# Softplus and the exponentials of one kernel through a single ScalarE table

## The chip, the cores and the metric

The kernel runs on one NeuronCore of a Trainium2 chip. The metric is device microseconds of one execution; before the change the median of 3 runs is 1014.26 us (1013.38 to 1015.45).

## What is computed

Three stages follow each other. The attention works on 4 batches of 8 heads, 576 tokens, head size 64:

```python
scores = q @ k.T / 8, causal; a = exp(scores - max); a /= a.sum() + 1e-9
local = a @ v
phi(x) = where(x > 0, x, exp(x) - 1) + 1
mem = (phi(q) @ M_prev) / (phi(q) . z_prev + 1e-6)
x = g * mem + (1 - g) * local              # g = sigmoid(beta), per head
```

The heads side by side give 2304 tokens of 512. The first layer is `h = x @ w_in` (512 to 2048), `g = max(h, 0) + log1p(exp(-|h|))`, which is softplus(h), and `g @ w_out` (2048 to 512). The second layer is `h = x @ w_in2`, a quotient of a cubic in h by `1 + |b0||h| + |b1| h^2`, and `@ w_out2`. All data is float32.

## The kernel before

Nothing is issued where it is written. Every call of an engine is recorded as an `Op` of a `Program` (line 392 of the profile is the one place that issues nearly all of them, which is why rows are told apart by tiles, not by lines). `Program.order` (a list scheduler) then walks through all recorded steps with modelled durations (`cost`), latencies between engines, a key per step (lower goes first) and dependencies by memory range; it fixes the order of each engine once, and also chooses the engine where a step was recorded with `flex` as possible on several. The order that comes out is static: an engine that waits holds back what stands behind it.

The attention runs in seven passes (`PASSES`) over batch and token range: three passes "L" (tokens 0 to 255, two units of 4 heads), one "F" (all 576 tokens, four units of 2 heads), three "H" (tokens 256 to 575, four units of 2 heads). The first three attention passes are done in float32 (`attention32`), the others with operands split into two float16 halves (`attention`, with `pre`, `scores`, `norm`). In a unit, `masked` (one DVE instruction) writes the masked scores and their minimum with the sign turned, `expo` (ACT) takes the exponential with that minimum as bias and sums it up, `norm` scales the rows and splits them, DMA transposes turn them, PE multiplies by v. A ring of three PSUM banks (`s_bank`) holds the scores.

The first layer goes over blocks of tokens, and over 8 pairs (`Q`) of 256 hidden columns each. `g1(Q)` multiplies into one PSUM bank `hf` and takes the activation; `g2(Q)` multiplies the result by `w_out`, three pairs later (`LAG` = 3). The first two blocks (16 pairs, 2 x 256 columns) are float32; the other 80 pairs (48 of 2 x 160 columns, 24 of 2 x 192, 8 of 2 x 256) take three float16 products. Attention of the next pass runs beside the first layer of the last one; PE takes steps of the attention ahead of those of the first layer.

The activation of a float16 pair takes, before: `Relu` (ACT or DVE) into SBUF; `Abs` with scale, `Exp`, `Ln` on ACT, in the bank; on DVE a multiply and add of the two parts, in the bank; a copy to float16 (the high half, ACT or DVE) and on DVE the difference (the low half). A float32 pair takes Relu, Abs, Exp, Ln and one DVE addition.

Weights are float64 in HBM and are turned to float32 by three bit steps of DVE on 128 x 512 (`bits`); 11 pieces of the second layer's weights are instead turned by `bits_abs`: two DVE steps, `Sign` and `Abs` on ACT, a product on POOL. Scales for the split come from sums of absolute values (`pre`, `w_scale`).

The second layer (`h1`, `h2_`) runs over 96 steps F of 128 hidden columns on 384 tokens each; each takes `Abs`, `Square`, `Ln` and `Exp` on ACT. `x2load` computes its constants from `fa`, `fb`, `fr`, which `consts2` makes from `a` and `b` with `Abs`, `Ln`, `Exp`. `w_split` splits its weights.

Of the kernel before, what the change touches and what calls it, by code (L numbers as in the profile page):

```python
# [24 lines left out]
LAG = 3  # L25

# [23 lines left out]
SIGN = ((0,), (0,))  # L50
SIGN2 = ((1,), (0, 0, 1))
# [5 lines left out]
SIGN3 = (0, 0, 1)  # L57
# [3 lines left out]
EXP = 0x7F800000  # L61

# [106 lines left out]
class Program:  # L169
# [5 lines left out]
    def __init__(self):  # L175
        self.ops = []
        self.access = {}
        self.key = 0.0
        self.pkey = 0.0
        self.bulk = False  # L180
        self.bias = BIAS
        self.cur = None

    def add(self, eng, name, fn, kw, writes=()):
# [29 lines left out]
        op.dma = dma  # L214
        if ported:
            op.port.add(eng)
# [205 lines left out]
def attn_moe_moe2(ctx, tc, q, k, v, m_prev, z_prev, beta, w1i, w1o, w2i, w2o, ca, cb, out):  # L422
# [147 lines left out]
    one = const.tile([128, 1], F32, name="one")  # L570
    pcnt = [0]
# [15 lines left out]
    def pow2(bound, n, name, bufs=3, out=None):  # L587

        cl = tn(name + "c", n, bufs) if out is None else out
        ts(cl, bound, 2.0 ** -13, 2.0 ** -53, ALU.mult, ALU.max)  # L590
        return cl, scale_of(cl, n, name, bufs)
# [131 lines left out]

    def pre(u):
# [3 lines left out]
        for i, src in enumerate((u.rq, u.rk, u.rv)):  # L728
            x = src.rearrange("p g d -> p (g d)")
            n = width(x)  # L730
            A.activation(out=u.nnf[:, 0:n], in_=x, func=AF.Abs, accum_out=acc[:, i:i + 1])
        A.activation(out=u.zt, in_=u.rq, func=AF.Relu, scale=-1.0)
        A.activation(out=u.ph, in_=u.zt, func=AF.Exp, scale=-1.0)
        stt(u.ph, u.rq, 0.0, u.ph, ALU.max, ALU.add)
# [6 lines left out]
        ts(rn, rn, 1e-6, None, ALU.add)  # L741
# [5 lines left out]
        ts(cl[:, 0:3], top[:, 0:3], 2.0 ** -13, 2.0 ** -53, ALU.mult, ALU.max)  # L747
# [22 lines left out]
        ts(tm, ut, m.e, None, ALU.mult)  # L770
# [35 lines left out]
    def expo(x, least, acc):  # L806
        A.activation(out=x, in_=x, func=AF.Exp, bias=least, scale=-1.0, accum_out=acc)


    def scores(u, e):  # L810
# [3 lines left out]
        if u.p.qts[0] == 0:  # L814
# [5 lines left out]
            for t in (1, 0):  # L820
                x = u.pr[e, t]
                masked(x, x, mask[:, 384 - t * 128:512], u.c, nm[:, t:t + 1])
                expo(x, nm[:, t:t + 1], sm[:, t:t + 1])
        for t in (2, 3):
# [6 lines left out]
            masked(x, x, mask[:, 384 - t * 128:512], u.c, nm[:, 0:1])  # L831
            expo(x, nm[:, 0:1], sm[:, t:t + 1])

    def scores_first(u):
# [4 lines left out]
        for t, es in ((1, (0, 1)), (1, (2, 3)), (0, (0, 1, 2, 3))):  # L839
# [5 lines left out]
            for e in es:  # L845
                x, c = u.pr[e, t], 4 * t + e
                masked(x, x, mask[:, 384 - t * 128:512], u.c, nm[:, c:c + 1])
                expo(x, nm[:, c:c + 1], sm[:, c:c + 1])

    def scores_last(u):  # L850
# [7 lines left out]
        masked(ds[1], ds[1], mask4, u.c, nm[:, 1:2], nm[:, 0:1])  # L858
        for j in range(2):
# [15 lines left out]
    def norm(u, e):  # L875
# [4 lines left out]
        ts(r[:, t0:t1], sm[:, t0:t1], 1e-9, u.isa[:, e:e + 1], ALU.add, ALU.mult)  # L880
# [123 lines left out]
    def attention32(u):  # L1004
# [12 lines left out]
        for t in (1, 0):  # L1017
# [7 lines left out]
            for e in range(4):  # L1025
# [3 lines left out]
                expo(x, nm[:, i:i + 1], sm[:, i:i + 1])  # L1029
        yield  # L1030
        A.activation(out=u.zt, in_=u.rq, func=AF.Relu, scale=-1.0)
        A.activation(out=u.ph, in_=u.zt, func=AF.Exp, scale=-1.0)
        stt(u.ph, u.rq, 0.0, u.ph, ALU.max, ALU.add)
# [5 lines left out]
        ts(rn, rn, 1e-6, None, ALU.add)  # L1039
# [4 lines left out]
        for t in (1, 0):  # L1044
            sl = slice(4 * t, 4 * t + 4)
            stt(r[:, sl], sm[:, sl], 1e-9, iog[:, h0:h0 + 4], ALU.add, ALU.mult)
# [37 lines left out]
    def xgroup(p):  # L1084
# [18 lines left out]
        g.csg = tn("xcsg")  # L1103
        ts(g.csg, g.c, g.sg, None, ALU.mult)
# [27 lines left out]
    def bits_abs(r, dst, sgn, acc=None):  # L1132


        hi, lo = r[:, :, 1], r[:, :, 0]
        m = dst.bitcast(U32)
        A.activation(out=sgn, in_=hi.bitcast(F32), func=AF.Sign)
        ts(m, hi, 3, 0xC0000000, ALU.logical_shift_left, ALU.bitwise_xor)
        stt(m, lo, 29, m, ALU.logical_shift_right, ALU.bitwise_or)
        A.activation(out=dst, in_=dst, func=AF.Abs, **({} if acc is None else {"accum_out": acc}))  # L1140
        G.tensor_tensor(out=dst, in0=dst, in1=sgn, op=ALU.mult)

    def w_scale(acc, name):
        m = tn(name + "m", 1, 1)
        V.tensor_reduce(out=m, in_=acc, axis=AX.X, op=ALU.max)
        bd, s = pow2(pmax(m, 1), 1, name, 1)
# [17 lines left out]
    def g1(Q):  # L1164
# [4 lines left out]
        r = vw(RR[Q % 2], (2 * tb,), F32)  # L1169
        if j < NF32:  # L1170

            for f in range(2):
# [73 lines left out]
    V.memset(one, 1.0)  # L1246
    V.memset(qe, 1.0)
# [86 lines left out]
    def w1_bits(which, pc):  # L1334
        r = w1_raw(which, pc)
        dst = w1_place(which, pc + 2, True)
        if SIGN[which][pc % len(SIGN[which])]:
# [334 lines left out]
```

## Time and profile before

| | |
|---|---|
| median of 3 runs | 1014.26 us (1013.38 to 1015.45) |
| span of the profiled execution | 1014.2 us, 22841 instructions |
| busy, share of the span | PE 95%, DVE 88%, ACT 82%, POOL 45% |
| granted TensorE clock, mean | 0.985 |

No time of the profiled execution other than its span is given; the span is within 0.1 us of the median of the runs. In the profile the float32 first layer shows from 43 to 234 us, the float16 first layer from 208 to 626 us, attention until 542 us and the second layer from about 623 us to the end. Names: "arena" is the one large SBUF tile, "tiny" holds columns of one to ten numbers, "bank" is PSUM, "a", "w", "lt", "gr" are further SBUF tiles.

### The profile page before, as it was taken

The page shows a single profiled execution, that of the slowest core. Times are in us where ns is not written, and L with a number is a line of the kernel's source. Part 1 is how long each engine was busy: PE and PEld are TensorE (multiplying, and loading weights), DVE is VectorE, ACT ScalarE, POOL GpSimd, SP SyncE. Part 2 cuts the span into 40 slices and gives each one's busy share as a digit, 9 for nine tenths or more (in the row PEclk, how much of TensorE's full clock was granted, in tenths as well). Part 3 has the DMA queues.
Part 4 walks back from the last instruction along what each step waited for, and adds up shares of the span by engine and source line. Part 5 has one row for each costly group of instructions (what it writes and reads, how often), then busy time and mean ns, then how long its engine had stood idle before and what let it go on. Part 6 is the DMA issues. An engine that isn't in the chain of part 4 may idle for free. (4 is left out here: it accounts for less than half of the span.)

```text
span 1014.2 us, 22841 instructions
## 1 busy us (share of the span) xinstructions
PE 959.6 (95%) x8256; PEld 696.0 (69%) x8256; DVE 893.1 (88%) x2193; ACT 826.8 (82%) x1934; POOL 455.6 (45%) x516
## 2 busy tenths in 40 slices
PE   7779999999979999999899999899999999999998
PEld 6547688788769888888888998445555555555553
DVE  6999778988899988899878999988989889798886
ACT  4886988888869999899887888867888787887875
POOL 3121566873342243342325343655655455555443
PEclk9969999999989999999999999989999999999999
DMA  9997347568689979998998664000001000000000
GB/s 249 317 227 200 66 102 145 123 121 158 130 170 168 153 144 163 184 182 193 209 282 267 219 207 144 1 1 32 32 1 63 1 32 32 1 32 2 32 1 31
DMA packets 249889, 122.08 MB, mean 120 GB/s; under 512 B 219184, under 2 KB 225328, under 8 KB 249776
## 3 DMA queue, kind: packets, MB, share of 16 engines
q1 hardware_dynamic: 249776, 120.63, 51.4%
q8 instruction: 64, 1.05, 0.4%
q14 instruction: 49, 0.40, 0.1%
HBM read 65.54 MB, written 15.73 MB: 80 GB/s over the span
## 5 line engine op out<-in xcount | busy, mean ns | idle before, releaser
L392 PE MATMUL bank<-arena,w 128*128 128x160 f16 (+3 forms) x4288 | 414.8, 256 | 12.0 <-DVE arena L392 7.3
L392 PE MATMUL bank<-arena 128*128 128x384 f16 (+10 forms) x2852 | 355.6, 299 | 24.3 <-DVE arena L392 8.6
L392 PEld LDWEIGHTS <-w 128*128 128x128 f16 x3840 | 292.8, 98 | 29.9 <-issue 18.7
L392 ACT ACTIVATE arena<-bank,tiny 128x384 f32<-128x384 f32 (+8 forms) x504 | 276.3, 587 | 41.4 <-PE bank L392 34.6
L392 PEld LDWEIGHTS <-arena 128*128 128x128 f16 (+1 forms) x2464 | 165.8, 105 | 119.8 <-issue 29.8
L392 POOL TENSOR_TENSOR arena<-arena 128x384 f32<-128x384 f32 (+8 forms) x165 | 167.9, 1021 | 166.3 <-ACT arena L392 104.1
L392 PE MATMUL bank<-arena,gr 128*128 128x512 f16 x864 | 202.8, 380 | 1.2 <-POOL gr L392 1.1
L392 PEld LDWEIGHTS <-gr 128*128 128x128 f16 x864 | 84.5, 98 | 95.5 <-POOL gr L392 2.5
L392 POOL TENSOR_TENSOR gr<-arena,gr 128x384 f16<-128x384 f32 x96 | 90.6, 944 | 103.6 <-issue 81.2
L392 POOL TENSOR_SCALAR arena<-arena,tiny 128x512 f16<-128x512 f32 (+9 forms) x94 | 71.6, 768 | 102.2 <-DVE tiny L392 31.9
L392 ACT ACTIVATE bank<-bank,tiny 128x320 f32<-128x320 f32 (+5 forms) x192 | 103.3, 545 | 14.5 <-DVE tiny L392 9.5
L392 ACT ACTIVATE bank<-bank 128x320 f32<-128x320 f32 (+2 forms) x208 | 104.8, 504 | 1.6
L392 ACT ACTIVATE arena<-bank 128x320 f16<-128x320 f32 (+5 forms) x147 | 72.2, 501 | 29.6 <-PE bank L392 16.6
L392 PEld LDWEIGHTS bank<-arena,w 128*128 128x128 f32 x448 | 83.1, 190 | 12.4 <-issue 1.5
L392 DVE SCALAR_TENSOR_TENSOR arena<-arena,tiny 128x512 f16<-128x512 f32 (+5 forms) x101 | 89.8, 903 | 1.8 <-POOL arena L392 1.1
L392 DVE SCALAR_TENSOR_TENSOR bank<-bank,tiny,lt 128x384 f32<-128x384 f32 x96 | 59.6, 621 | 34.0 <-ACT lt L392 32.3
L392 ACT ACTIVATE lt<-arena,qe 128x384 f32<-128x384 f32 x96 | 59.0, 614 | 32.6 <-POOL arena L392 31.0
L392 DVE SCALAR_TENSOR_TENSOR arena<-arena,qe,lt 128x384 f32<-128x384 f32 x96 | 76.0, 791 | 0.7 <-ACT lt L392 0.7
L392 DVE SCALAR_TENSOR_TENSOR arena<-bank,tiny,arena 128x384 f16<-128x384 f32 (+4 forms) x112 | 64.0, 591 | 8.9 <-ACT arena L392 8.4
L392 DVE TENSOR_SCALAR tiny<-tiny 128x1 f32<-128x1 f32 (+8 forms) x349 | 64.5, 208 | 6.4 <-ACT bank L392 5.1
L392 DVE CUSTOM_DVE_ANT_0 bank<-bank,mask,tiny 128x384 f32<-128x384 f32 (+4 forms) x112 | 66.8, 605 | 2.4 <-PE bank L392 2.0
L392 PEld LDWEIGHTS bank<-arena 128*128 128x128 f32 (+3 forms) x412 | 43.2, 168 | 29.2 <-ACT arena L392 8.1
(122 smaller groups left out, 1143.3 us busy)
## 6 DMA issues: line engine op xcount, KB each, us to landing
arena<-in_moe_w_out_dram SPq DMA_DIRECT2D x32, 512.0 KB, 5.0
arena<-in_moe_w_in_dram SPq DMA_DIRECT2D x24, 512.0 KB, 5.1
w2d<-a SPq DMA_DIRECT2D x24, 256.0 KB, 3.0
arena<-w2d SPq DMA_DIRECT2D x24, 256.0 KB, 4.6
arena<-in_k_dram SPq DMA_DIRECT2D x44, 128.0 KB, 3.1
arena<-in_v_dram SPq DMA_DIRECT2D x44, 128.0 KB, 2.9
arena<-arena SPq DMA_DIRECT2D x32, 160.0 KB, 2.9
arena<-x2d SPq DMA_DIRECT2D x6, 768.0 KB, 4.3
```

The source lines that it names most:

```text
L392: fn(**{k: (v.fn() if isinstance(v, Lazy) else v) for k, v in kw.items()})
```

## The change

Softplus(x) is now one ACT instruction, from another activation table. The exponentials of softmax and of phi use the same table: with 18 subtracted ahead, softplus(x - 18) equals e^-18 e^x to a relative 1e-8 for x <= 0, and the factor e^-18 (`EOFF`) cancels in the quotients or is multiplied out. ACT has one table at a time, so two further table loads are recorded as steps (`tables`): the first comes after every Exp and Abs of the start (those of `consts`) and ahead of every Softplus, the second after the last Softplus and ahead of every Ln, Exp and Abs of the second layer and of `consts2`. Where minima were used as bias, a new step `lower` (DVE or POOL, by the scheduler's choice) subtracts 18 from them, for several score tiles together in `scores_first`, `attention32` and for t = 0, 1 in `scores`. Scales come from sums of squares, whose root is bounded by a shift of the number's bits (`half_bits`, DVE); `bits_abs` is gone, and all pieces take the three steps of `bits`.

```diff
+    def tables(self, load):
+        last = None
+        for name, ops in zip(TABLES, self.of_table):
+            if last is not None:
+                op = self._new()
+                op.key = -1e9
+                op.eng = "ACT"
+                op.alts["ACT"] = [1300.0, [(lambda name=name: load(name), {})]]
...
+    def half_bits(x):
+        ts(x.bitcast(U32), x.bitcast(U32), 1, None, ALU.logical_shift_right)
+    def feature(u):
+        A.activation(out=u.zt, in_=u.rq, func=AF.Relu, scale=EOFF)
+        A.activation(out=u.ph, in_=u.rq, func=AF.Softplus, bias=off)
+        stt(u.ph, u.ph, EOFF, u.zt, ALU.min, ALU.add)
     def expo(x, least, acc):
-        A.activation(out=x, in_=x, func=AF.Exp, bias=least, scale=-1.0, accum_out=acc)
+        A.activation(out=x, in_=x, func=AF.Softplus, bias=least, scale=-1.0, accum_out=acc)
+    def lower(x):
+        P.flex(*[(e, "tensor_scalar", dict(out=x, in0=x, scalar1=OFF, scalar2=None, op0=ALU.subtract)) for e in (V, G)])
...
             masked(x, x, mask[:, 384 - t * 128:512], u.c, nm[:, 0:1])
+            lower(nm[:, 0:1])
             expo(x, nm[:, 0:1], sm[:, t:t + 1])
...
...
-            P.flex(
-                (A, "activation", dict(out=r, in_=hf, func=AF.Relu)),
-                (V, "tensor_scalar", dict(out=r, in0=hf, scalar1=0.0, scalar2=None, op0=ALU.max)),
-            )
-            A.activation(out=hf, in_=hf, func=AF.Abs)
-            A.activation(out=hf, in_=hf, func=AF.Exp, scale=-1.0)
-            A.activation(out=hf, in_=hf, func=AF.Ln, bias=1.0)
-            tt(vw(GH[Q % NGH], (2 * tb,), F32), hf, r, ALU.add, "V")
+            A.activation(out=vw(GH[Q % NGH], (2 * tb,), F32), in_=hf, func=AF.Softplus)
...
-        P.flex(
-            (A, "activation", dict(out=r, in_=hf, func=AF.Relu, scale=g.csg)),
-            (V, "tensor_scalar", dict(out=r, in0=hf, scalar1=0.0, scalar2=g.csg, op0=ALU.max, op1=ALU.mult)),
-        )
-        A.activation(out=hf, in_=hf, func=AF.Abs, scale=g.c)
-        A.activation(out=hf, in_=hf, func=AF.Exp, scale=-1.0)
-        A.activation(out=hf, in_=hf, func=AF.Ln, bias=1.0)
-        stt(hf, hf, g.sg, r, ALU.mult, ALU.add)
         gh = vw(GH[Q % NGH], (2, 2 * tb), F16)
-        scopy(gh[:, 0], hf, None, "AV")
-        tt(gh[:, 1], hf, gh[:, 0], ALU.subtract, "V")
+        A.activation(out=hf, in_=hf, func=AF.Softplus, scale=g.c)
+        scopy(gh[:, 0], hf, g.sg, "AV")
+        stt(gh[:, 1], hf, g.sg, gh[:, 0], ALU.mult, ALU.subtract)
```

How the order moves. At the start of the program ACT had, before, the eight exponentials of the first attention unit (a_98, a_99, with tiny as bias) ahead of the Exp and Abs of `consts` (gg, bb):

```order
L392 ACTIVATE arena<-bank_69 128x512
L392 ACTIVATE arena<-arena 128x512 x2
L392 ACTIVATE a_98,tiny<-a_98,tiny 128x256 x2
L392 ACTIVATE a_99,tiny<-a_99,tiny 128x256 x2
L392 ACTIVATE a_98,tiny<-a_98,tiny 128x128 x2
L392 ACTIVATE a_99,tiny<-a_99,tiny 128x128 x2
L392 ACTIVATE arena<-arena 128x512
L392 ACTIVATE gg<-gg 128x8
L392 ACTIVATE bb<-bb 128x2
```

With the change, gg and bb come first, then the table load, then one sum of squares, then the eight:

```order
L426 ACTIVATE arena<-bank_69 128x512
L426 ACTIVATE gg<-gg 128x8
L426 ACTIVATE bb<-bb 128x2
L196 ACT_TABLE_LOAD
L426 ACTIVATE a_99,wacc<-w_4_82 128x512
L426 ACTIVATE a_98,tiny<-a_98,tiny 128x256 x2
L426 ACTIVATE a_99,tiny<-a_99,tiny 128x256 x2
L426 ACTIVATE a_98,tiny<-a_98,tiny 128x128 x2
```

The eight now stand behind two DMA transfers (beta and b) and the load. On POOL, in the passes "H", the place before held the work of the next unit's `pre` alone:

```order
L392 TENSOR_TENSOR arena<-arena,tiny 128x384
L392 TENSOR_SCALAR arena<-arena 128x6x64
L392 TENSOR_TENSOR arena<-arena 128x6x64
L392 TENSOR_SCALAR arena<-arena,tiny 128x10x64
L392 TENSOR_TENSOR arena<-arena 128x192 x2
```

Now the step `lower` (tiny<-tiny, one column) stands between its pieces:

```order
L426 TENSOR_TENSOR arena<-arena,tiny 128x384
L426 TENSOR_SCALAR tiny<-tiny 128x1
L426 TENSOR_SCALAR arena<-arena 128x6x64
L426 TENSOR_TENSOR arena<-arena 128x6x64
L426 TENSOR_SCALAR tiny<-tiny 128x1
L426 TENSOR_SCALAR arena<-arena,tiny 128x10x64
L426 TENSOR_SCALAR tiny<-tiny 128x1
L426 TENSOR_TENSOR arena<-arena 128x192 x2
```

Of all the steps of this kind POOL has 66, DVE the rest. At the seam of the two layers, ACT with the change goes from the last Softplus (bank_73) through the load and `consts2` (fa, tiny) to the last output copies of the first layer and the first step of the second (bank_70, 384 wide); before, `consts2` stood far ahead, in the first tenth of the program:

```order
L426 ACTIVATE bank_73<-bank_73,tiny 128x320
L196 ACT_TABLE_LOAD
L426 ACTIVATE fa<-aa 128x4
L426 ACTIVATE tiny<-fr 128x2
L426 ACTIVATE tiny<-tiny 128x2
L426 ACTIVATE arena<-bank_68,tiny 128x320
L426 ACTIVATE arena<-bank_69,tiny 128x320
L426 ACTIVATE arena<-bank_70,tiny 128x384 x2
```

On DVE there, the splits of the second layer's output weights (arena<-arena,tiny 128x512) now stand partly ahead of the steps that wait for `fa`; before, all 16 came after the second layer's first step:

```order
L426 SCALAR_TENSOR_TENSOR arena<-bank_72,tiny,arena 128x320
L426 SCALAR_TENSOR_TENSOR arena<-arena,tiny 128x512 x2
L426 TENSOR_SCALAR arena<-bank_73,tiny 128x320
L426 SCALAR_TENSOR_TENSOR arena<-bank_73,tiny,arena 128x320
L426 SCALAR_TENSOR_TENSOR arena<-arena,tiny 128x512
L426 TENSOR_SCALAR tiny<-tiny,fa 128x1 x3
L426 SCALAR_TENSOR_TENSOR tiny<-tiny 128x1
```

Nine of the 16 splits stand ahead of that wait.

## Rows read from the trace of the kernel before

**Rows 1.** Page of the profile, part 1: busy us (share of the span) x instructions.
```profile
PE 959.6 (95%) x8256; PEld 696.0 (69%) x8256; DVE 893.1 (88%) x2193; ACT 826.8 (82%) x1934; POOL 455.6 (45%) x516
```

**Rows 2.** Windows: stretch, length, PE, PEld, DVE, ACT, POOL busy (x), PEclk, DMA share, GB/s.
```profile
0.00:60.00 60.00, 43.88 (x312) 33.04 (x312) 50.51 (x150) 40.95 (x124) 13.40 (x24) 0.97 1.00 275
60.00:130.00 70.00, 65.01 (x370) 47.46 (x370) 62.87 (x189) 56.73 (x161) 24.54 (x32) 0.91 0.61 156
130.00:270.00 140.00, 138.63 (x1033) 113.31 (x1032) 121.05 (x322) 119.51 (x288) 83.86 (x89) 1.00 0.67 127
270.00:300.00 30.00, 24.00 (x272) 19.27 (x270) 28.03 (x78) 19.98 (x51) 14.03 (x18) 0.89 0.77 172
300.00:420.00 120.00, 117.50 (x1502) 105.77 (x1502) 106.57 (x340) 111.41 (x284) 36.00 (x54) 1.00 0.89 156
420.00:580.00 160.00, 146.27 (x2113) 134.14 (x2110) 140.66 (x377) 138.45 (x355) 59.38 (x67) 1.00 0.94 225
580.00:640.00 60.00, 59.08 (x727) 52.65 (x725) 57.73 (x125) 50.39 (x121) 24.47 (x28) 1.00 0.50 159
640.00:700.00 60.00, 55.73 (x283) 28.25 (x282) 54.91 (x84) 43.32 (x85) 34.74 (x36) 0.94 0.00 1
700.00:960.00 260.00, 259.66 (x1400) 136.80 (x1399) 228.42 (x466) 209.83 (x406) 140.53 (x148) 1.00 0.07 25
```

**Rows 3.** By form, ACT: names, shapes, xcount | busy us, mean ns | idle before.
```profile
L392 ACT ACTIVATE bank<-bank 128x320 f32<-128x320 f32 x96 | 42.4, 443 | 0.9
L392 ACT ACTIVATE bank<-bank 128x512 f32<-128x512 f32 x64 | 38.4, 600 | 0.5
L392 ACT ACTIVATE bank<-bank 128x384 f32<-128x384 f32 x48 | 24.0, 500 | 0.3
L392 ACT ACTIVATE arena<-bank 128x320 f16<-128x320 f32 x48 | 21.2, 442 | 11.6 <-DVE bank L392 11.3
```

**Rows 4.** By form, DVE: the first layer's last steps.
```profile
L392 DVE SCALAR_TENSOR_TENSOR bank<-bank,tiny,arena 128x320 f32<-128x320 f32 x48 | 26.4, 551 | 4.1 <-ACT bank L392 3.9
L392 DVE TENSOR_TENSOR arena<-bank,arena 128x320 f16<-128x320 f32 x48 | 23.1, 482 | 4.0 <-ACT arena L392 3.8
L392 DVE TENSOR_TENSOR arena<-bank,arena 128x512 f32<-128x512 f32 x16 | 10.8, 681 | 1.4 <-ACT bank L392 1.4
```

**Rows 5.** By form, DVE and POOL: one-column steps and a weight step.
```profile
L392 DVE TENSOR_SCALAR tiny<-tiny 128x1 f32<-128x1 f32 x116 | 20.9, 189 | 0.5 <-ACT bank L392 0.2
L392 POOL CROSS_LANE_REDUCE tiny<-tiny 128x1 f32<-128x1 f32 x18 | 6.9, 382 | 22.0 <-DVE tiny L392 21.9
L392 DVE SCALAR_TENSOR_TENSOR a<-arena,a 128x512 uint32<-128x512 uint32 x40 | 32.1, 804 | 0.2
```

**Rows 6.** Waits of PE, 270 to 300 us: who for whom, total us, times, longest.
```profile
PE bank L392 <- DVE arena L392: 3.4, 2, 3.2
PE bank L392 <- POOL arena L392: 1.9, 1, 1.9
```

**Rows 7.** Waits of PE, 420 to 580 us.
```profile
PE bank L392 <- DVE arena L392: 5.4, 6, 1.5
PE bank L392 <- DMA arena<-arena: 4.6, 4, 1.9
```

**Rows 8.** By form, ACT: the one table load.
```profile
L1245 ACT ACT_TABLE_LOAD x1 | 1.3, 1283 | 0.7 <-PEq L1656 0.7
```

**Rows 9.** Timelines, start of the program, DVE and ACT: start us, us, what, idle before.
```profile
14.53 0.51 ACT L392 ACTIVATE a<-a,tiny 128x256 f32<-128x256 f32 x1 [1.45 <-DVE tiny L392]
18.57 0.19 ACT L392 ACTIVATE gg<-gg 128x8 f32<-128x8 f32 x1
18.70 0.69 DVE L392 SCALAR_TENSOR_TENSOR arena<-arena 128x512 f32<-128x512 f32 x1 [0.40 <-DMA bb<-in_moe_b_dram]
24.40 0.22 DVE L392 SCALAR_TENSOR_TENSOR tiny<-tiny,iog 128x4 f32<-128x4 f32 x2
```

**Rows 10.** Waits of PE, 640 to 700 us.
```profile
PE bank L392 <- DVE arena L392: 4.0, 2, 3.2
```

More of the change, by code (lines that the diff above doesn't have):

```diff
@@ L182, in __init__, with _table @@
         self.cur = None
+        self.table = 0
+        self.of_table = [[], [], []]
+    def tables(self, load):
[6 more added lines that the diff above has]
+                op.alts["ACT"] = [1300.0, [(lambda name=name: load(name), {})]]
+                for q in last:
+                    q.succ.add(op.idx)
+                op.npred = len(last)
+                op.succ.update(q.idx for q in ops)
+                for q in ops:
+                    q.npred += 1
+            last = ops
+    def _table(self, op, kw):
+        f = kw.get("func")
+        if f == AF.Softplus:
+            i = 1
+        elif f in (AF.Abs, AF.Sign, AF.Exp, AF.Ln):
+            i = self.table
+        else:
+            return
+        if op not in self.of_table[i]:
+            self.of_table[i].append(op)
     def add(self, eng, name, fn, kw, writes=()):
@@ L214, in add @@
         op.dma = dma
+        if eng == "ACT":
+            self._table(op, kw)
         if ported:
@@ L584, in pmax, with pow2 @@
         return r
-    def pow2(bound, n, name, bufs=3, out=None):
-        cl = tn(name + "c", n, bufs) if out is None else out
-        ts(cl, bound, 2.0 ** -13, 2.0 ** -53, ALU.mult, ALU.max)
+    def pow2(bound, n, name, bufs=3, k=1.0):
+        cl = tn(name + "c", n, bufs)
+        ts(cl, bound, k * 2.0 ** -13, 2.0 ** -53, ALU.mult, ALU.max)
         return cl, scale_of(cl, n, name, bufs)
@@ L730, in pre @@
             n = width(x)
[L731 to L734, printed above, removed]
+            A.activation(out=u.nnf[:, 0:n], in_=x, func=AF.Square, accum_out=acc[:, i:i + 1])
+        half_bits(acc[:, 0:3])
+        feature(u)
         for e in range(nh):
@@ L822, in scores @@
                 masked(x, x, mask[:, 384 - t * 128:512], u.c, nm[:, t:t + 1])
[L823 removed]
+            lower(nm)
+            for t in (1, 0):
+                expo(u.pr[e, t], nm[:, t:t + 1], sm[:, t:t + 1])
         for t in (2, 3):
@@ L1028, in attention32 @@
                 masked(x, bks[e % 2][:, e // 2 * n:e // 2 * n + n], mask[:, 384 - t * 128:512], -0.125, nm[:, i:i + 1])
-                expo(x, nm[:, i:i + 1], sm[:, i:i + 1])
+            for e0 in range(0, 4, NLOW):
+                lower(nm[:, 4 * t + e0:4 * t + e0 + NLOW])
+                for e in range(e0, e0 + NLOW):
+                    i = 4 * t + e
+                    expo(pr[e][:, 128 * t:128 * t + n], nm[:, i:i + 1], sm[:, i:i + 1])
         yield
-        A.activation(out=u.zt, in_=u.rq, func=AF.Relu, scale=-1.0)
-        A.activation(out=u.ph, in_=u.zt, func=AF.Exp, scale=-1.0)
-        stt(u.ph, u.rq, 0.0, u.ph, ALU.max, ALU.add)
+        feature(u)
         th = lambda x: x.rearrange("p (t h) d -> p t (h d)", t=2)
@@ L1145, in w_scale @@
         V.tensor_reduce(out=m, in_=acc, axis=AX.X, op=ALU.max)
-        bd, s = pow2(pmax(m, 1), 1, name, 1)
+        half_bits(m)
+        bd, s = pow2(pmax(m, 1), 1, name, 1, ROOT)
         inv = tn(name + "i", 1, 1)
@@ L1336, in w1_bits @@
         dst = w1_place(which, pc + 2, True)
-        if SIGN[which][pc % len(SIGN[which])]:
-            bits_abs(r, dst, a_t[0][:, 768 + pc % 2 * 256:1024 + pc % 2 * 256].bitcast(BF16), wacc1[which][:, pc:pc + 1])
-        else:
-            bits(r, dst.bitcast(U32))
+        bits(r, dst.bitcast(U32))
     def w1_stage2(which):
         for pc in range(16):
-            if not SIGN[which][pc % len(SIGN[which])]:
-                A.activation(out=a_t[1][:, 768:1280], in_=w1_place(which, pc + 2, True), func=AF.Abs, accum_out=wacc1[which][:, pc:pc + 1])
+            A.activation(out=a_t[1][:, 768:1280], in_=w1_place(which, pc + 2, True), func=AF.Square, accum_out=wacc1[which][:, pc:pc + 1])
         bd, s, inv = w_scale(wacc1[which], f"w1{which}")
@@ L1357, in attn_moe_moe2, with w2_bits @@
     w2q = vw(TT[0], (512,), F32)
-    def w2_bits(which, pc, r, dst, sgn, tmp, sign):
+    def w2_bits(which, pc, r, dst, tmp):
         acc = wacc[:, 32 + pc:33 + pc] if which else None
-        if sign:
-            bits_abs(r, dst, sgn, acc)
-        else:
-            bits(r, dst.bitcast(U32))
-            if which:
-                A.activation(out=tmp, in_=dst, func=AF.Abs, accum_out=acc)
+        bits(r, dst.bitcast(U32))
+        if which:
+            A.activation(out=tmp, in_=dst, func=AF.Square, accum_out=acc)
         if which == 0:
@@ L1486, in attn_moe_moe2 @@
             ts(bd, bd, 2.0 ** -100, None, ALU.max)
-            A.activation(out=bd, in_=bd, func=AF.Ln)
-            A.activation(out=bd, in_=bd, func=AF.Exp, scale=0.5)
+            half_bits(bd)
+            ts(bd, bd, ROOT, None, ALU.mult)
             _, w2.s = pow2(bd, 1, "w2i", 1)
```

49 lines of the change are left out of this document (24 added, 25 removed).

## The prediction

> **What bounds the kernel now.** I read the page's first part, then windows by stage, then the forms of ACT and DVE, then what PE waited for. PE is busy 95% of the span, DVE 88%, ACT 82% [rows 1]. The share alone decides nothing, so look at the stages [rows 2]. From 700 to 960 us, the second layer, PE is busy 259.66 of 260 us at full clock: there nothing can be won by lighter ACT or DVE work, and the change leaves that layer's steps alone. What can be won is PE's idle time ahead of it, 60 us less 43.88, and so on down the rows: 16.1 us up to 60, 5.0 from 60 to 130, 1.4 from 130 to 270, 6.0 from 270 to 300, 2.5 from 300 to 420, 13.7 from 420 to 580, 0.9 from 580 to 640, 4.3 from 640 to 700: 50 us in all. To this comes the clock, which is at times granted at its lower level of 1.2 GHz: means of 0.97, 0.91, 0.89 and 0.94 are 1.8, 6.3, 3.3 and 3.6 us of full speed lost, all in stretches in which PE stood idle, too. About 65 us is thus the whole reserve. In the same stretches the other engines are nearly full: DVE 28.03 of 30 us from 270 to 300, ACT 111.41 of 120 from 300 to 420, DVE 140.66 and ACT 138.45 of 160 after that. So up to 640 us PE, ACT and DVE limit each other, and PE is ahead only by little.
>
> The Trainium skill (Perfetto Trace Analysis, Identifying the Most-Contended Engine) says that a matmul's busy share is no good measure of how near PE is to its limit, since pipelined matmuls look otherwise than they are. If so, some waiting hides inside PE's busy time, and the reserve before 640 us is more than the idle time; no row here gives that part, and my sum leaves it out.
>
> **ACT.** Per float16 pair, Abs with scale becomes Softplus with scale (same operands), and the Relu with scale gives its place to the scaled copy. Exp, Ln and the unscaled copy are gone. By form [rows 3]: 96 steps of 320 columns (42.4 us) and 48 of 384 (24.0) go whole; of the 64 with 512 columns 16 belong to float16 pairs and 48 to the float32 ones (38.4 us, all gone); the copies are 48 x 0.442 = 21.2 us, and the 32 wider ones at least 0.442 each, 14.1. That is 140 us off ACT. It gains two table loads at 1.283 us [rows 8], 2.6 us. ACT is busy 538 us up to 640 us [rows 2] and falls to about 400: it is no longer near its limit anywhere.
>
> The Trainium skill (ScalarE: Activation LUTs, What ACT_TABLE_LOAD costs) puts a switch of tables at 2.66 us, as a drain comes to the load. By that the two would be 5.3 us, and the sum 2.7 us worse if both were on PE's path. The row shows the load alone, at the start, where nothing ran before it.
>
> **DVE.** The multiply and add of the pair's two parts is gone: 48 x 0.551 = 26.4 us and 32 wider ones at no less, 17.6; so are the 16 additions of the float32 pairs, 10.8 us [rows 4]. The last difference becomes a multiply and subtract: 80 times 0.551 for 0.482, 5.5 us more. Added: eight more bit steps at 0.8 us, 6.4, and some 50 one-column steps (`half_bits`, part of `lower`) at 0.19, 9.5 [rows 5]. Net 33 us less of 567 up to 640 us. DVE stays the second busiest.
>
> **POOL.** It takes 66 steps `lower`. No row shows a one-column step of that kind on POOL; below stands DVE's 0.189, above the cross-lane maximum of one column, 0.382 [rows 5]. I take 0.38, 25 us, as POOL's own row is nearer. POOL is busy 36 of 120 and 59 of 160 us in the stages with most of them [rows 2], so its time is covered; what counts is the link, since the exponential now waits for DVE, then POOL.
>
> **What PE gets of it.** Stage by stage:
> - 270 to 300 us. This is the start of the pass with 576 tokens, whose attention is just in time; PE waits 3.4 us on DVE and 1.9 on POOL [rows 6], with DVE full. DVE has by then lost the 16 additions (10.8 us) and eight wide multiply-adds, and ACT the 38.4 us of steps with 512 columns [rows 3]. Of 6.0 idle and 3.3 of clock I take 7; ends 0 and 9.3.
> - 300 to 580 us. 16.2 us idle. PE's waits from 420 to 580 name DVE with 5.4 us and the DMA transposes with 4.6 [rows 7]. The DVE ones are the low halves of a pair, whose chain loses three steps and about 1.4 us (0.443 x 2 and 0.551); the transposes come only as early as the softmax ahead of them. I take 9; ends 0 and 16.2.
> - 130 to 270 and 580 to 640 us. 2.3 us idle; I take 1.
> - Up to 130 us. The eight first exponentials began at 14.53 us [rows 9]. With the change they stand behind gg and bb, and the wait for bb's transfer ended at 18.70; with 0.2 for the two small steps and 1.28 for the load they start at about 20.2, 5.7 us later. But what needs their sums came only at 24.40, as it waited for 1 - g, too. The eight and one step more were done when gg started at 18.57, so the eight take at most 4.0 us and end at about 24.2: the delay just fits. The float32 pairs' lighter work gives a few us. I take 2 gained; ends 5.7 lost and 10 gained (of 29 idle and clock).
> - 640 to 700 us, the seam. 4.3 us idle, 4.0 of them on DVE [rows 10], and 3.6 of clock. Nine of the 16 weight splits move ahead, which empties DVE. Against that, the second layer's constants now wait for the last Softplus, the load, `fa` and the exponential of `consts2`, and with them some 25 one-column steps on DVE at 0.19 (4.8 us) and about four splits at 0.8 (3.2). Four g2 of 24 matmuls (727 in 60 us while PE is full: 0.082 us each, at most 2.0 a piece) and four h1 (1400 in 260 us: 0.186 each, 2.2 for 12) cover 16.8 us of that chain. The chain is an estimate: 0.5 for the Softplus, 1.9 for the load and three small steps, 8 on DVE, and some 5 for the eight steps of a first h1 activation at the 0.6 of such a step [rows 4], 15.4. I take nothing either way; ends 7.9 gained and 6 lost (the present loss again).
>
> Sum: 7 + 9 + 1 + 2 = 19 us off the span of 1014.2: **995 us**. The span stands within 0.1 us of the median of the runs, 1014.26, so the same holds for the median.
>
> **Rivals.**
> 1. *PE was the bound, nothing moves.* The Trainium skill (Perfetto Trace Analysis, Optimization Strategy) says to work on the most contended engine first; by that rule ACT's 140 us are worth nothing. As a mechanism here: PE's idle time would come from transposes and from the fixed order, not from ACT and DVE. For it speaks that 4.6 us of waits name DMA [rows 7] and that DVE sheds only 6%; against it, 5.4 and 3.4 us name DVE [rows 6, 7], and ACT was over 90% full from 300 to 420. Time 1012 to 1016, that is, within 0.2%, about what a measurement of this kernel can tell from no change.
> 2. *The new link makes softmax late: slower.* `lower` on POOL stands behind products like the present ones; a wait of one such step, about 1 us, and 0.38 for itself, give 1.4 us per link. The 16 float16 units of two heads have two links each that nothing else covers: 16 x 2 x 1.4 = 45 us of longer chain. PE hides it as long as pairs of the last block are left; if over half of it shows (21 us), the gain is gone. With two thirds shown: 995 + 30 = 1025. Against it: the planner counts these steps in its order, ACT's queue is empty enough to take the exponential at once, and POOL is idle over 60% there.
> 3. *The barriers bite.* Both ends of the table loads show: 5.7 us at the start and 6 at the seam, with the lower clock after them. Then 995 + 12 = 1007.
> 4. *Attention runs ahead.* With ACT at 62%, attention of a pass is done before the last pass's pairs, and PE fills all gaps from 130 to 640 us (27.8 us with the clock) and half of what is lost at the seam and before 130: 1014 - 28 - 4 - 7 = 975.
> 5. *The new function costs more per column.* Abs, Exp and Ln stand in one form and average the same; the bound is a step 10% dearer on 96 of them, 5 us of ACT that is idle anyway. That the order shows three table loads in all excludes more switches. It changes no chance.
>
> **Chances.** The forecast with its bounds, 987 to 1003: 0.46. Rival 4, 968 to 987: 0.16. Rival 3 or half the gain, 1003 to 1012: 0.18. No change: 0.09. Slower: 0.11. So faster 0.80, same 0.09, slower 0.11. The range from 976 to 1014 leaves out about 0.06 below and 0.14 above.
>
> **What would show it.** Right: ACT's busy time falls to about 690 us and DVE's to about 860; PE's idle from 270 to 580 halves; the low clock near 285 us is gone; the second layer still runs without gaps and starts about 19 us earlier. Wrong: first exponentials that hold up DVE or PE past 25 us, a gap of PE of over 8 us at the second table load, or POOL named as what ACT waits for all through the attention; and if PE's idle time stays where it is with ACT and DVE relaxed, rival 1 holds.

## The result and the profile after

The changed kernel takes 1024.29 us (median of 4 runs, 1021.95 to 1026.89) against 1014.86 for the kernel before on the same chip: ratio 1.010, 95% interval 1.0073 to 1.0128. The forecast was 995, faster. The profiled execution has a span of 1023.2 us, 9.0 more than before.

Part 1 of the page of the changed kernel answers to [rows 1]:

```profile
PE 963.7 (94%) x8256; PEld 701.5 (69%) x8256; DVE 863.2 (84%) x2162; ACT 713.6 (70%) x1626; POOL 476.3 (47%) x573
```

ACT lost 113 us and DVE 30, with as many matmuls. The work was taken away as forecast, and yet the time rose. The windows, with the columns of [rows 2], show where:

```profile
0.00:60.00 60.00, 45.89 (x302) 33.86 (x303) 43.67 (x142) 34.17 (x99) 24.63 (x25) 0.93 0.96 263
60.00:130.00 70.00, 54.56 (x302) 36.51 (x301) 63.72 (x202) 54.71 (x160) 25.12 (x35) 0.82 0.63 161
130.00:270.00 140.00, 137.45 (x940) 113.11 (x939) 107.44 (x290) 91.71 (x226) 79.10 (x94) 1.00 0.60 119
270.00:300.00 30.00, 29.56 (x358) 24.52 (x357) 28.21 (x95) 20.48 (x50) 14.49 (x24) 1.00 0.85 154
300.00:420.00 120.00, 113.70 (x1408) 100.42 (x1406) 100.21 (x319) 87.82 (x224) 45.37 (x78) 0.99 0.92 165
420.00:580.00 160.00, 148.63 (x2136) 138.29 (x2134) 138.82 (x365) 100.90 (x244) 60.65 (x80) 0.99 0.98 235
580.00:640.00 60.00, 56.65 (x787) 56.15 (x785) 50.01 (x102) 25.43 (x58) 23.87 (x28) 0.97 0.45 143
640.00:700.00 60.00, 58.77 (x332) 31.61 (x330) 53.18 (x108) 47.75 (x93) 34.45 (x36) 1.00 0.02 6
700.00:960.00 260.00, 260.00 (x1404) 137.24 (x1402) 228.66 (x465) 206.57 (x399) 140.71 (x148) 1.00 0.06 22
```

PE's loss in a stage is its idle time and what the lower clock took: length less busy, and length times (1 less PEclk). From 60 to 130 us that was 5.0 + 6.3 before [rows 2] and is 15.4 + 12.6 now: 17 us are lost there. From 270 to 300 and from 640 to 700 us the loss shrank from 9.3 to 0.4 and from 7.9 to 1.2, and from 300 to 640 it grew from 17.1 to 25.6. Over all stages it is 65 before and 76 now; the difference, 11, is the 9 of the span within the rounding of PEclk.

The loss from 60 to 130 us leads back to one chain. Before, piece 14 of the first layer's W1-in (bit steps named arena<-arena of uint32 belong to pieces 14 and 15 of the two weights) had its last step on DVE at 66.79 us, and the third float32 pair (the matmuls arena,w of 256 columns in float32) began on PE at 79.01:

```profile
66.79 0.68 DVE L392 SCALAR_TENSOR_TENSOR arena<-arena 128x512 uint32<-128x512 uint32 x1
79.01 1.89 PE L392 MATMUL bank<-arena,w 128*128 128x256 f32 x8
```

In the changed kernel the same stands in the timelines of DVE, ACT and PE as follows (start us, us, what, idle before):

```profile
111.87 0.69 DVE L426 SCALAR_TENSOR_TENSOR arena<-arena 128x512 uint32<-128x512 uint32 x1
112.81 1.29 DVE L426 SCALAR_TENSOR_TENSOR arena<-arena 128x512 uint32<-128x512 uint32 x2
...
114.22 1.45 ACT L426 ACTIVATE arena<-bank 128x512 f32<-128x512 f32 x3
...
114.85 1.99 PE L426 MATMUL bank<-arena,w 128*128 128x256 f32 x8 [1.83 <-ACT arena L426]
```

The first of the two steps at 112.81 is piece 14's last, done at 113.5. Raw pieces 14 and 15 lie in `GH`, the slots into which the float32 pairs write their results. The first Softplus cannot write before piece 14 is decoded, its bank stays full, and with two banks for the pairs the third pair waits: at 114.85 in place of 79.01. The last matmul of that name starts at 245.5 us in place of 225.6. That the pieces and not something else hold the pairs is what e1 tests. PE does all that the attention gives it from 60 to 114 us, which does not fill it.

### The profile page after: what moved, and what is told of

Read it like the earlier page. It is cut to its first block, busy times and chain, and to the rows that moved or that the text cites. A ratio compares the mean times of both kernels' runs of the same rounds, so it can differ in the third digit from the quotient of the medians.

```text
span 1023.2 us, 22600 instructions
## 1 busy us (share of the span) xinstructions
PE 963.7 (94%) x8256; PEld 701.5 (69%) x8256; DVE 863.2 (84%) x2162; ACT 713.6 (70%) x1626; POOL 476.3 (47%) x573
## 5 line engine op out<-in xcount | busy, mean ns | idle before, releaser
L426 PE MATMUL bank<-arena 128*128 128x384 f16 (+13 forms) x2852 | 356.1, 301 | 25.7 <-DVE arena L426 8.6
L426 ACT ACTIVATE arena<-bank,tiny 128x384 f32<-128x384 f32 (+9 forms) x508 | 271.1, 581 | 57.6 <-PE bank L426 31.8
L426 PEld LDWEIGHTS <-w 128*128 128x128 f16 x3840 | 293.5, 98 | 16.2 <-issue 6.9
L426 POOL TENSOR_TENSOR arena<-arena 128x384 f32<-128x384 f32 (+7 forms) x166 | 171.8, 1038 | 138.4 <-ACT arena L426 84.6
L426 ACT ACTIVATE bank<-bank,tiny 128x512 f32<-128x512 f32 (+5 forms) x192 | 102.1, 535 | 73.7 <-PE bank L426 40.1
L426 DVE SCALAR_TENSOR_TENSOR arena<-bank,tiny,arena 128x384 f16<-128x384 f32 (+5 forms) x192 | 109.2, 589 | 34.1 <-ACT arena L426 31.3
L426 POOL TENSOR_SCALAR arena<-arena,tiny 128x512 f16<-128x512 f32 (+9 forms) x100 | 78.6, 791 | 92.2 <-DVE tiny L426 39.5
L426 DVE SCALAR_TENSOR_TENSOR arena<-arena,tiny 128x640 f16<-128x640 f32 (+5 forms) x100 | 82.9, 844 | 6.8 <-POOL arena L426 5.1
L426 DVE TENSOR_SCALAR tiny<-tiny 128x1 f32<-128x1 f32 (+9 forms) x396 | 71.7, 207 | 13.3 <-ACT bank L426 9.4
L426 POOL TENSOR_SCALAR tiny<-tiny 128x1 f32<-128x1 f32 (+2 forms) x66 | 19.3, 293 | 92.8 <-DVE tiny L426 86.5
L426 DVE SCALAR_TENSOR_TENSOR bank<-arena,tiny,bank 128x384 f32<-128x384 f32 x96 | 59.2, 617 | 2.2 <-ACT arena L426 0.8
```

Of the source, the lines that this page charges most:

```text
L426: fn(**{k: (v.fn() if isinstance(v, Lazy) else v) for k, v in kw.items()})
```

## The experiments

The first four ask what of the start costs: the order, the barrier of the table load, or the new step `lower`.

**Pieces first (e1).** Only the priority of two pieces changes:

```diff
-        P.key = KEY_W1I + pc * 0.1
+        P.key = (KEY_W1I if pc < 14 else 24) + pc * 0.1
```

> The changed kernel with one number changed: the decoding of pieces 14 and 15 of the first layer's W1-in gets the priority 24 (ahead of W1-out's pieces) in place of 41.4 and 41.5. Theory (the order): in the changed kernel the first Softplus of the float32 pairs stands still until 114.2 us, because its result goes into the slot in which raw piece 14 still waits for DVE (decoded at 114.1; before, at 67.5), so that pairs 2 and later start 20 to 35 us late and PE is busy 54.6 of 70 us from 60 to 130 in place of 65.0. With the pieces decoded early pair 2 starts near 60 us, PE is busy 63 us or more from 60 to 130, and the whole takes 1007 to 1014 us (1024.3 less 10 to 17). Rival (the barrier and the softmax links are the loss): pair 2 moves, but PE's idle time stays in other waits, and the time stays at 1020 to 1026.

Measured: 1020.13 us (1018.75 to 1023.34), ratio to before 1.0066 (1.0039 to 1.0092). Timelines of DVE and PE, then the windows:

```profile
43.49 1.30 DVE L426 SCALAR_TENSOR_TENSOR arena<-arena 128x512 uint32<-128x512 uint32 x2
...
56.99 1.99 PE L426 MATMUL bank<-arena,w 128*128 128x256 f32 x8
```

```profile
60.00:130.00 70.00, 68.60 (x413) 51.80 (x412) 59.95 (x184) 55.23 (x165) 20.87 (x28) 1.00 0.56 146
130.00:270.00 140.00, 133.35 (x1033) 109.43 (x1032) 124.88 (x334) 96.62 (x237) 89.17 (x104) 1.00 0.67 130
270.00:300.00 30.00, 19.95 (x212) 13.63 (x211) 26.13 (x83) 19.68 (x49) 15.57 (x23) 0.77 0.90 188
```

The chain holds: decoded at 44, the third pair at 57, PE full at full clock from 60 to 130. The time does not follow: 4 us gained where 10 to 17 were expected, and 1020 lies in the rival's range, which said just this, that the pair would move and the idle time stay in other waits. From 270 to 300 us PE is now idle for 10.1 us and loses 6.9 more to the clock, waiting above all for what the DMA transposes bring (PE's waits from 255 to 300 us: in total, times, longest):

```profile
PE bank L426 <- DMA arena<-arena: 5.4, 4, 2.5
PE bank L426 <- DVE tiny L426: 2.4, 2, 1.8
```

The pairs were done early, and the attention of the 576-token pass, whose tokens come next, was not: its 49th masked product (the first of that pass) starts at 146.1 us, in the changed kernel at 135.9. The two go together in all runs of this series whose last matmul of the pairs starts before 228 us: where that product starts at 134 to 137 us (before, e2, e8, e9) PE loses 1.3 to 9.3 us from 270 to 300, where it starts at 143 to 149 (e1, e3, e7, e10, e12) it loses 15.6 to 23.1. So what PE needs at 290 us is the later of two streams, pairs and attention, and both want DVE. No run moves the attention alone, so that is argued from these runs and not tested.

**No first barrier (e2), and both (e3).** The exponential and absolute value of the start become Relus, the softplus table is the one loaded first, and the load after the start goes. The gate and two constants of the second layer are thus not what they should be; all else is computed. Of the edit, the two Relus:

```diff
...
-        A.activation(out=gg, in_=gg, func=AF.Exp, scale=-1.0)
+        A.activation(out=gg, in_=gg, func=AF.Relu, scale=-1.0)
...
-        A.activation(out=bb, in_=bb, func=AF.Abs)
+        A.activation(out=bb, in_=bb, func=AF.Relu)
...
```

> The changed kernel without its first table load: the softplus table is the one loaded at the start. The exponential of the gate becomes a Relu and the absolute value of the two constants a Relu as well, so that these two constants are wrong or right by chance; all else is computed. Theory (the order): the 5.7 us by which the first exponentials are late are not lost themselves, but push piece 13 and 14 behind W1-out's; without them the order by itself has piece 14 decoded near 50 us, pair 2 starts near 60 us, and the time is 1007 to 1014, no better than with the pieces put first and the barrier left in. Rival (the barrier itself costs): the time is the same 1007 to 1014 or less, but the barrier with pieces first stays above 1018.

> Both edits above at once (no first table load, with the Relus in place of exponential and absolute value; pieces 14 and 15 decoded first). What this gains over the pieces alone is the barrier's own price. Theory (the order): within 3 us of the pieces alone. Rival (barrier): 5 us or more below it.

Measured: 1007.41 us without the barrier (ratio 0.9933, 0.9908 to 0.9958), 1014.39 with both edits (0.9997, 0.9981 to 1.0013). PE's timeline without the barrier:

```profile
55.85 1.99 PE L426 MATMUL bank<-arena,w 128*128 128x256 f32 x8
```

The barrier alone tips the order: without it the third pair starts at 55.8 us and 17 us come back, though what it adds by itself is 1.3 us of a load and 7.5 of delay to the first exponentials. With the pieces first its price is 5.7 us (1020.13 less 1014.39; the two intervals leave some 3 us either way). By their numbers both runs came out as the rival had it: e2 at the low end of 1007 to 1014 with the pieces-first kernel above 1018, and e3 over 5 us below that kernel. So the barrier costs more than the order of the pieces alone. And the pieces first, which gained 4 with the barrier, lose 7 without it: an edit's worth turned its sign with the order around it. That the barrier's price is no fixed sum either shows in e9 below, which has it, starts its first exponentials at 21.25 us and takes 998.4.

**`lower` on DVE alone (e4).**

```diff
-for e in (V, G)])
+for e in (V,)])
```

> The changed kernel with the subtraction of the offset (lower) allowed on DVE alone; POOL has none of the 66 steps. Rival (the link over POOL makes the softmax late, 6.1 us of one wait of ACT on POOL at 52 to 58 us and many smaller ones): the time falls to 1014 or less. Theory (the order at the start): pair 2 still waits for piece 14 past 100 us, and the time stays between 1020 and 1028.

Measured: 1038.26 us, ratio 1.0235 (1.0211 to 1.0259), worse than both expected. The third pair still starts at 114.4, so the link over POOL is not what holds it. But with `lower` on another engine all is ordered anew, so the 14 us above the changed kernel are no price of the link. From 640 to 700 us PE waits 7.8 us once for DVE. Windows of this run:

```profile
60.00:130.00 70.00, 52.92 (x283) 37.25 (x284) 57.56 (x184) 51.77 (x151) 20.61 (x25) 0.73 0.58 148
640.00:700.00 60.00, 52.16 (x331) 30.29 (x329) 49.44 (x114) 39.41 (x78) 28.22 (x33) 0.91 0.06 20
```

**The orders exchanged (e5, e6).** To part steps from order, each kernel's steps were issued in the other's order, which is given as a list of places in the kernel (left out here):

```diff
...
-        for o in self.order():
+        for o in self.given():
```

> The changed kernel's own steps, issued in the order of the kernel before: each step that both have stands on its engine where it stood before, a removed step leaves no gap, an added one (lower, half_bits, the third bit step of a piece, the table loads) comes right behind what it needs; on POOL and DVE as in the changed kernel. Theory (the order cost it, not the steps): the time is below before's 1014.9, by the 5 to 19 us of which the prediction spoke: 996 to 1010 us, and pair 2 of the float32 ones starts near 79 us again. Rival (the steps cost it: lower's link, the barriers): 1018 us or more in the old order as well.

> The kernel before with its own steps, issued in the order that the changed kernel's planner gave: steps that both have stand where they stand in the changed kernel, Abs, Exp, Ln, Relu and the multiply-add come right behind what they need. No table load, no lower. Theory (the order cost it): the start loses its 20 us here too, and the time is 1025 to 1045 us. Rival (the steps cost it): within 5 us of before, 1010 to 1020.

Measured: 1104.94 us (ratio 1.088, 1.0823 to 1.0939) and 1247.75 us (1.230, 1.2277 to 1.2327). Both lie outside what either theory expected. PE's waits on what DVE brings to the arena, over the whole program, in e5 and then in e6:

```profile
PE bank L564 <- DVE arena L564: 75.0, 48, 14.1
```

```profile
PE bank L536 <- DVE arena L536: 75.2, 39, 5.6
```

The theories are not told apart: a foreign order costs 9 to 23%, far more than what is looked for, whichever way it goes. An order fits the durations it was made from, and steps and order cannot be exchanged singly. The fair question is what the change is worth when both kernels are ordered by the same rules, for several sets of rules.

**Three pairs under other keys (e7 to e10, e12).** e7 is the kernel before with the edit of e1. e8 and e9 are the kernel before and the changed one with three priorities changed; the set was taken from plans that the program's scheduler made of many sets, as the one with the shortest plan of the kernel *before* (the plans are not shown here):

```diff
-KEY_W1I = 40
+KEY_W1I = 30
-KEY_U2 = -10
+KEY_U2 = -20
-        P.key = KEY_W1I + pc * 0.1
+        P.key = (KEY_W1I if pc < 14 else 24) + pc * 0.1
```

e10 and e12 are the changed kernel and the one before with the transfers of beta, a and b issued first, and the edit of e1:

```diff
-    (lambda: load(u[0], 0, 1), lambda: load(u[1], 0, 1)),
+    (consts, lambda: load(u[0], 0, 1), lambda: load(u[1], 0, 1)),
     (lambda: load(u[0], 2), batch),
-    (consts,),
+    (),
```

> The kernel before with the edit of the first experiment: pieces 14 and 15 of W1-in decoded at priority 24. Its partner is the changed kernel with the same edit, 1020.1 us. Theory (the change is worth 10 to 19 us under keys that favour neither; the present keys happen to suit the old durations): the kernel before loses its good order and takes 1025 to 1045 us, more than its partner. Rival (the steps themselves cost 5 to 10 us, under any keys): 1008 to 1016 us, less than its partner.

> The kernel before with three other priorities: pieces of W1-in at 30 in place of 40, pieces 14 and 15 at 24, attention units from the third on ahead by 20 in place of 10. Partner: the changed kernel with the same three. Theory (the change is worth 10 to 19 us): 1000 to 1015 us, and the partner 10 to 19 us below it. Rival (the steps cost): the partner stands above it by 5 to 10 us.

> The changed kernel with the same three priorities as the run before this one; every result is computed as in the changed kernel. Theory: pairs and attention of the 576-token pass are both in time, 985 to 1000 us, below both kernels as they are. Rival: 1010 us or more.

> The changed kernel with the transfers of beta, a and b put first in the queue (the first table load no longer waits for the one that landed at 19.9 us) and pieces 14 and 15 decoded early. The barrier stays, but is passed some 5 us earlier. Theory (order): like the pieces alone within some 8 us, 1010 to 1022 us, since the start is no longer the bound once the pairs are in time. Rival (the barrier's 5.7 us are lost one to one): 1012 to 1016 us, as without the barrier.

> The kernel before with the transfers of beta, a and b first and pieces 14 and 15 decoded at priority 24. Partner: the changed kernel with the same two edits, 1016.6 us. Theory (the change is worth 10 to 20 us under keys that favour neither kernel): 1027 to 1040 us. Rival (the two pairs so far are chance): 1010 to 1018 us.

| keys | before, us | changed, us | change |
|---|---|---|---|
| as they are | 1014.9 | 1024.3 | +9.4 |
| pieces first (e7, e1) | 1039.8 | 1020.1 | -19.6 |
| three priorities (e8, e9) | 1013.6 | 998.4 | -15.2 |
| transfers and pieces first (e12, e10) | 1037.5 | 1016.6 | -20.9 |

The intervals of the ratios to before are at most 0.4% wide to either side, and no two of a line overlap. In three of four sets the change gains 15 to 21 us (by the ratios 1.5 to 2.0%; the partners of the second and fourth line ran on different chips), in the set that the kernel came with it loses 9. The three are not independent: all have the pieces first, which costs the kernel before 25 us by itself (e7). The fairest single number is the best measured of each, e9 against e8, 15 us; that no set suits the old steps better is not shown. e7, e8, e9 and e12 came out in the ranges of their theories, as did e10, whose range the rival's overlaps. In e10 the eight exponentials start at 16.72 us in place of 22.07, and the time is 3.5 us below e1's. e9 beats both kernels: ratio 0.9848 (0.9808 to 0.9888), and it leaves nothing out. Its page, the start of its third pair and four of its windows:

```profile
PE 951.8 (95%) x8256; PEld 692.5 (69%) x8256; DVE 864.6 (87%) x2170; ACT 710.4 (71%) x1618; POOL 469.5 (47%) x570
```

```profile
59.85 1.89 PE L426 MATMUL bank<-arena,w 128*128 128x256 f32 x8
```

```profile
60.00:130.00 70.00, 68.37 (x412) 51.54 (x411) 65.66 (x205) 55.35 (x165) 28.64 (x31) 1.00 0.64 167
...
270.00:300.00 30.00, 28.67 (x336) 25.03 (x335) 27.07 (x87) 21.30 (x53) 15.04 (x23) 1.00 0.93 189
...
420.00:580.00 160.00, 148.58 (x2172) 139.23 (x2170) 135.49 (x332) 94.69 (x228) 58.19 (x74) 1.00 0.91 244
...
640.00:700.00 60.00, 60.00 (x325) 31.53 (x323) 53.03 (x93) 47.52 (x90) 33.75 (x36) 1.00 0.04 14
```

Its partner e8, with the steps of the kernel before (the profiled execution is the slowest of its ten, 1018.25 us):

```profile
60.00:130.00 70.00, 61.43 (x343) 45.02 (x342) 61.68 (x190) 54.27 (x153) 26.60 (x32) 0.85 0.59 159
...
270.00:300.00 30.00, 24.72 (x263) 19.67 (x258) 24.51 (x73) 21.70 (x53) 12.10 (x16) 0.89 0.81 152
...
420.00:580.00 160.00, 145.61 (x2050) 134.97 (x2045) 138.72 (x348) 128.16 (x330) 56.06 (x61) 0.97 0.85 218
```

In e9 both streams are in time: the third pair starts at 59.9 us, the 576-token pass at 137.0, and PE is idle 1.3 us from 270 to 300. Engine totals are nearly those of the changed kernel: not the work differs, but its order. The kernel before wins nothing by this set (e8: ratio 1.000, 0.998 to 1.002), though there, too, the third pair starts early, at 54.0 us.

The links over POOL can be read in these runs, too. ACT's waits on POOL's small steps up to 640 us, with the bank of the scores, in the changed kernel and in e9:

```profile
ACT bank L426 <- POOL tiny L426: 24.1, 23, 4.6
```

```profile
ACT bank L426 <- POOL tiny L426: 23.0, 18, 2.4
```

The same 23 to 24 us of waits stand in a kernel of 1024 and in one of 998 us: they are not what parts the two.

**Another slot for the transposed softmax (e11).** The last two float32 pieces of W1-in lie in `TT` until the pairs are done, and the odd units of the 576-token pass need `TT`:

```diff
-        a = vw(TT[0], (768,), F32) if u.i % 2 else a_t[1][:, 0:768]
+        a = vw(RR[0], (768,), F32) if u.i % 2 else a_t[1][:, 0:768]
```

> The changed kernel, keys as they are, with one place changed: the transposed softmax of the odd units goes into the slots RR that the old Relu used and that are free now, in place of TT, where the last two float32 pieces of W1-in lie until the last float32 pair (245 us) is done. Theory (the late pairs hold up the attention of the 576-token pass): its rows 75 to 88 of masked products, which stood from 209 to 245 us, go on without that hole; the first pair of that pass starts 5 to 10 us earlier than 299, and the time is 1012 to 1020 us. Rival (DVE and the chains set that attention's end, and the hole is only order): the hole closes, the first pair stays within 3 us of 299, and the time stays within 5 us of 1024.

Measured: 1030.16 us, ratio 1.0150 (1.0121 to 1.0178). The hole closes: masked products 74 and 75 start at 211.4 and 211.6 us (in the changed kernel at 209.2 and 236.0), and the pass's last at 252.8 (269.5). The time rises by 6 all the same, and the pass's first pair (first matmul of 192 columns) starts at 302.5 us, after 297.4 in the changed kernel. Neither the theory nor the rival had that. PE in that run:

```profile
60.00:130.00 70.00, 52.69 (x284) 34.42 (x283) 61.49 (x189) 52.05 (x154) 22.47 (x31) 0.78 0.59 152
130.00:270.00 140.00, 135.51 (x908) 110.01 (x908) 119.00 (x343) 97.19 (x246) 84.67 (x103) 1.00 0.66 132
270.00:300.00 30.00, 28.30 (x334) 23.86 (x333) 24.79 (x71) 16.94 (x39) 13.89 (x20) 1.00 0.70 137
```

The hole was real, and closing it could give back little: once the pairs are late, PE is full from 115 to 300 us (3.0 us idle of 170 from 130 on in the changed kernel, by its windows), so an earlier attention only stands in line. What PE lost before 115 us could not be made up there. The 6 us more are another order again: the third pair starts at 116.4 us, and from 60 to 130 us PE loses 32.7 us in place of 28.0.

## Why the prediction was wrong

- **Engine totals: right for DVE (863 for 860), nearly for POOL, ACT off.** `lower` took 0.28 us for one column on POOL, forecast 0.38. ACT fell to 713.6, not 690: the sum took each removed step at its own duration, but successive steps of ACT overlap, as 22.07 with 0.49 and the next at 22.47 in the rows below, and busy time counts the overlap once. (The durations of all of ACT's steps fell by 162.5 us, its busy time by 113.) The sum had DVE's added bit steps as eight; they are eleven. Forms of POOL and DVE, with busy us and mean ns:

```profile
L426 POOL TENSOR_SCALAR tiny<-tiny 128x1 f32<-128x1 f32 x55 | 15.4, 280 | 70.4 <-DVE tiny L426 64.1 <-DVE tiny L441 5.0
...
L426 DVE SCALAR_TENSOR_TENSOR arena<-bank,tiny,arena 128x320 f16<-128x320 f32 x48 | 26.1, 544 | 6.9 <-ACT arena L426 6.8
```

- **"Up to 130 us ... I take 2 gained; ends 5.7 lost and 10 gained": this step failed.** The first exponentials started at 22.07 us (14.53 before [rows 9]), where 20.2 was forecast: bb's transfer was done only at 19.93, and a sum of squares, 0.63 us, stands ahead of them, which the working left out:

```profile
19.93 0.20 ACT L426 ACTIVATE bb<-bb 128x2 f32<-128x2 f32 x1 [2.33 <-DMA bb<-in_moe_b_dram]
20.15 1.28 ACT L196 ACT_TABLE_LOAD   x1
21.44 0.63 ACT L426 ACTIVATE a<-w 128x512 f32<-128x512 f32 x1
22.07 0.49 ACT L426 ACTIVATE a<-a,tiny 128x256 f32<-128x256 f32 x1
22.47 0.19 ACT L426 ACTIVATION_READ_ACCUMULATOR a<-a,tiny 128x1 f32 x1
```

  That is 7.5 us for the 5.7 named, and up to 130 us 17.1 us were lost (29.2 to 46.3, idle and clock) where 5.7 was the worst end. What failed is the assumption that a delay costs at most itself. The order is made anew from the durations; with the delay, DVE's steps of piece 14 fell from 67 to 113 us, behind W1-out's, and a delay of 7.5 us became 20 at the last float32 matmul. The bound was taken from the old order shifted, and of the new order at the start ACT's alone was read. DVE's order around the two pieces that lie in `GH` would have shown it.
- **"270 to 300 us: 7."** The loss there fell by 8.9 us, but since the pairs came late and PE had work in plenty. Where both streams are in time it fell by 8.0 (9.3 to 1.3 in e9), the size forecast. That DVE's lost steps are the reason is not shown: with the same steps the loss there is 16.9 in e1 and 15.6 in e10.
- **"300 to 580 us: 9", "130 to 270 and 580 to 640 us: 1".** Not seen. From 300 to 580 us the loss stayed, 16.2 before, 20.5 in the changed kernel, 16.5 in e9; against e8, in its slowest run, it fell by 6.2 (22.7 to 16.5). From 130 to 270 and 580 to 640 us e9 loses 7.2 more than before. With ACT relaxed, other waits came up: in the changed kernel PE waits from 420 to 580 us for DVE as before [rows 7], and 4.8 us for the maxima that POOL hands to PE:

```profile
PE bank L426 <- DVE arena L426: 5.0, 3, 4.0
PE bank L426 <- POOL tiny L426: 4.8, 3, 2.0
```

- **The seam: forecast 0, ends 7.9 and -6.** It gained 6.7 (7.9 to 1.2), and 7.9 in e9. In the changed kernel and in e9 the covers were enough; in e4, under another order, 13.2 us were lost here. The second load came right behind the last Softplus:

```profile
634.54 0.50 ACT L426 ACTIVATE bank<-bank,tiny 128x320 f32<-128x320 f32 x1 [2.26 <-PE bank L426]
635.06 1.28 ACT L196 ACT_TABLE_LOAD   x1
636.35 0.21 ACT L426 ACTIVATE fa<-aa 128x4 f32<-128x4 f32 x1
```

  The Trainium skill (ScalarE: Activation LUTs, What ACT_TABLE_LOAD costs) puts a switch at 2.66 us; here 1.31 us lie between the end of the last Softplus (635.04) and `fa`, so here, by the measurement, a switch costs hardly more than the load.
- **Rivals.** Rival 2 named 1025, and 1024.3 came, but by luck: its sign is there, ACT waiting 24.1 us for POOL, but the same waits stand in e9, at 998.4, and with all its steps on DVE the third pair is as late (e4). Rival 3, the barrier at its own price (1007), is the nearest in kind: the barrier was the trigger, and 5.7, its price with the pieces first, is what it gave for the start; of its 6 at the seam nothing came, and that the barrier tips the order was no case of mine. Rival 1 leaned on the Trainium skill (Perfetto Trace Analysis); the rule to optimize the most contended engine first stands there in Identifying the Most-Contended Engine, not in Optimization Strategy, and it does not say that time on another engine is worth nothing. Three pairs of runs with equal matmuls and 15 to 21 us between them speak against that reading. Rival 4 did not come: from 130 to 640 us e9 loses 27.2 us, before 27.8. Its own sum does not add up either, as half of the 29 us lost before 130 is 14 and not 7. Rival 5 is out: the Softplus with scale took 498 ns for 320 columns, the Abs in its place 507.
- **The size.** 19 us were forecast; under the three other sets the change is worth 15 to 21. That the two agree is luck. In e9 PE loses 17.6 us less than before, but with 9.0 gained up to 130 us (forecast 2), 8.0 from 270 to 300 (7), 0.3 lost from 300 to 580 (9 gained), 7.2 lost from 130 to 270 and 580 to 640 (1 gained) and 7.9 gained at the seam (0). No case allowed for the priorities that came with the old durations no longer to fit; the range ended at 1014 for that reason.

## What to carry to other kernels

Where a scheduler makes the order from durations, a lighter step is a new order, and priorities alone moved these kernels by 2.6% (1013.6 to 1039.8 us with the old steps, 998.4 to 1024.3 with the new): time a change under several sets of priorities, on both sides, before it is judged, and choose them again after it is made. In the new order, read for each slot that two uses share who must let go of it, and where that step now stands on its engine. In the changed kernel, a loss ahead of a stretch in which the fullest engine had no idle time stayed lost.

## What the runs showed of the hardware that was not expected

The granted clock, a mean of the levels 1.2 and 2.4 GHz, mostly went down with PE's busy time from 60 to 130 us: 1.00 with PE busy 68.6 and 68.4 of 70 us (e1, e9), 0.91 with 65.0 [rows 2], 0.85 with 61.4 (e8), 0.82 with 54.6 (the changed kernel), 0.78 and 0.73 with 52.7 and 52.9 (e11, e4). So with the 10.4 us more that PE stood idle there in the changed kernel, another 6.3 went by the clock. It is not the stretch's own idle time alone: e7 and e10 are equally busy (67.95 and 67.99 us), and e7 has 0.92, e10 1.00. In e7 the lower level was granted from 54.7 to 71.8 us, and PE had been busy 5.5 us of the ten from 50 to 60.

One product on POOL, whose like takes 1.0 to 1.6 us, stands in the changed kernel's timeline with 11.35:

```profile
42.74 11.35 POOL L426 TENSOR_TENSOR arena<-arena,gg 128x512 f32<-128x512 f32 x1 [2.99 <-DMA arena<-in_M_prev_dram]
```

In e1 the same one has 10.48 us. Most of it may be waiting inside the instruction; on what, no run here was made to tell. It is not what makes the pairs late: in e4 and e11 the same product takes 1.04 us, and the third pair is as late. The price of the barrier by itself, apart from the order, stays open: 5.7 us is the difference of two kernels whose orders differ, too, and stands for one set of keys.
